# Block-causal attention into an RWKV channel mix: a second batch's q and k in nine-token rows, transposed by TensorE, with a new table of ranks

## The chip, the cores and the metric

The kernel runs on one core of one Trainium2 chip. The metric is the device time of one execution in microseconds, median over runs. All inputs and the output are in HBM as fp32. The kernel before took 289.88 us (three runs, 289.01 to 291.78) when the prediction was made. Executions of one kernel differ by about 1%, so small differences below come with a 95% interval. A run counts as slow when it took over 1.5% more than the fastest of its kernel; ratios use fast runs alone. "Slower" and "faster" below mean that the interval lies on one side of 1; a change clear of 2% is shown only where the whole interval lies beyond 0.98 or 1.02.

## The reference, cut to what matters

Attention over 8 batches, 8 heads, 576 tokens, head size 64, with a mask of blocks of 64 tokens; its output goes through a token-shift channel mix (d_model 512, d_ff 1024).

```python
scores = q @ k.T / 8                                  # (8, 8, 576, 576)
scores = where(pos_i // 64 >= pos_j // 64, scores, -1e9)
x = softmax(scores) @ v                               # heads side by side: (8, 576, 512)
x_prev = x shifted by one token, zero at each batch's start
xk = mu_k * x + (1 - mu_k) * x_prev
xr = mu_r * x + (1 - mu_r) * x_prev
out = sigmoid(xr @ w_r) * (relu(xk @ w_k) ** 2 @ w_v) # w_k 512x1024, w_v 1024x512, w_r 512x512
```

q, k and v are normal numbers times 0.1. The scores are therefore all close to zero.

## The kernel before

Each batch goes through the same steps: q and k are loaded as fp32, cast to bf16, and transposed so that the head dimension lies on the partitions; TensorE makes scores, ScalarE the exponentials, TensorE the product with v and a transpose back, GpSimd and VectorE the token-shift mixes. The 4608 tokens are then taken in nine chunks of 512 through WK, WR and WV.

The order of every engine is fixed when the kernel is built. A list scheduler in the kernel takes tasks with modelled lengths, dependences and buffer rings; on each engine it takes the ready task of lowest rank. The ranks come from a table that has been tuned by search.

```python
class Plan:
    LATENCY = {"PE": 0.12, "ACT": 0.08, "DVE": 0.08, "POOL": 0.1, "SP": 2.4}
    ...
RANK = {
 'loads': ['v0', 'g1q', 'v3', 'g0k', 'g0q', 'wk4', 'wr3', 'wk5', 'v1', ...],  # the order of the first loads
 ...
 'qk': [47.0, 48.0, 50.5, 52.5], 'v': 56.0, 'turn': -176.0, 'av': -44.5,      # the steady part, per batch
 'xt': 8.5, 'mix': 694.5, 'xr': 29.5, 'moe': 20.0,
}
```

Batches 1 to 7 use the DMA crossbar. Each pair of heads takes two half loads for q and two for k, in rows of 256 B (64 fp32), a cast of each half on GpSimd, a cast of the tail (the last 64 of 576 tokens), and a transposing DMA that SyncE issues:

```python
def add_qk(b, pr, rank, turn_rank):
    for n, src in enumerate((q, k)):
        t = load(key, lambda: new("ld", [P, 4, 2, D], FP),
                 lambda d, src=src: [
                     (d[:, :, h], src[b, 2 * pr + h, 0:512].rearrange(
                         "(t p) d -> p t d", p=P)) for h in range(2)], ...)
        ... nc.gpsimd.tensor_copy(tiles["nb", b, pr][:, n, 0:4], ...)
    last = on("POOL", 0.4, rank, tail, ...)
    ... nc.sync.dma_start_transpose(out=tiles["qkt", b][:, pr]..., in_=tiles["nb", b, pr]...)
```

Batch 0 is the exception. Its q and k come as rows of nine tokens (2304 B), two blocks of two heads in one tile, are cast by sixteen instructions that each take half of the partitions (every second one moves its data to the other half), and are transposed by TensorE:

```python
LONG = {(0, 0): ("DVE", "POOL", "DVE", "ACT"), ...}
def add_long(g, ranks):
    ... d[:, x], src[0, 4*g + 2*x:4*g + 2*x + 2].rearrange("y (p j) d -> (y p) (j d)", j=JT) for x in range(2)
    for i, (x, y) in enumerate(((0, 0), (1, 1), (1, 0), (0, 1))):
        dst = tiles["nb", 0, g, n][x * D:x * D + D, :, y * D:y * D + D]
        src = tiles[key][y * D:y * D + D, x].rearrange("p (j d) -> p j d", d=D)
```

GpSimd also makes two of a chunk's four shift differences (t_d), the fp16 casts of v (VO), and a small "fix" of xk and xr at each batch's first token (128x4). The fix comes after the mixes of its chunk, and the chunk's WK matmuls need it.

The softmax here doesn't subtract the row's maximum and nothing guards it: scores larger than these inputs give would overflow.

## Time and profile before

| | before |
|---|---|
| time, median | 289.88 us |
| span of the profiled run | 287.3 us |
| TensorE busy (instructions) | 253.5 us (2260) |
| VectorE, ScalarE, GpSimd busy | 207.9, 187.9, 142.3 us |
| packets under 512 B | 142848 of 151071 |
| first matmul of each chunk's WV product, chunks 0 to 8 | 61.5, 98.4, 124.2, 153.3, 181.0, 212.4, 238.3, 257.8, 275.3 us |

"Busy" TensorE isn't TensorE at its full rate.

SyncE's own queue in order of time (start us, length, issued DMA) shows when batch 2's first load, its tail, goes out, and the weight load ahead of it:

```profile
52.24 3.23 SPq L226 DMA_DIRECT2D t_ld<-in_moe_w_v_dram  x1
55.51 0.61 SPq L226 DMA_DIRECT2D t_tl<-in_q_dram  x1
```

GpSimd's timeline at the end of the hole around 75 to 81 us (start, length, instruction, in brackets the idle time before it and its releaser):

```profile
79.86 0.61 POOL L358 CAST VO<-t_vl 128x512 f16<-128x512 f32 x1 [1.37 <-DMA t_vl<-in_v_dram]
80.44 0.65 POOL L695 TENSOR_TENSOR t_xk<-t_xt,MUK 128x4 f16<-128x4 f32 x1
```

### The profile page before, as it was taken

What the parts mean: (1) busy time and instruction counts of PE and PEld (TensorE: products, weight loads), DVE (VectorE), ACT (ScalarE), POOL (GpSimd) and SP (SyncE); (2) the same over time, 40 slices, a digit from 0 to 9 for tenths busy, and PEclk for the clock granted to TensorE, in tenths of its full rate; (3) what the DMA queues carried; (4) which work ended last, traced back from release to release, by engine and by line L of the source; (5) the groups of instructions that cost most, each with busy time, mean ns of one, the idle gap of its engine ahead of it and who ended that gap; (6) DMA issues with size and microseconds to landing.
All of it is one profiled execution on the core that took longest, in us unless ns stands there. A gap on an engine that the chain in (4) does not pass through costs nothing.

```text
span 287.3 us, 6211 instructions
## 1 busy us (share of the span) xinstructions
PE 253.5 (88%) x2260; PEld 137.2 (48%) x2260; DVE 207.9 (72%) x356; ACT 187.9 (65%) x297; POOL 142.3 (50%) x310
## 2 busy tenths in 40 slices
PE   0366948989679999999999989999999999999994
PEld 0333722455325644565565445556545655444441
DVE  4661696485968598868989856878787789897641
ACT  1368576875748768857886677867866884360530
POOL 5546374455647665567577357755864221301000
PEclk9999995999979999999999999999999999999998
DMA  7997899999999999999989998999899100201102
GB/s 218 361 248 175 226 191 216 267 177 234 180 216 177 192 257 253 193 203 235 255 172 184 227 264 179 186 263 239 178 212 255 40 3 37 110 2 74 72 37 113
DMA packets 151071, 52.59 MB, mean 183 GB/s; under 512 B 142848, under 2 KB 142848, under 8 KB 151040
## 3 DMA queue, kind: packets, MB, share of 16 engines
q1 hardware_dynamic: 151040, 52.19, 84.0%
q8 instruction: 18, 0.29, 0.5%
q14 instruction: 13, 0.11, 0.1%
HBM read 33.56 MB, written 9.44 MB: 150 GB/s over the span
## 4 chain that ended last, share of the span: by engine, by line
PE 53%; DMA 16%; DVE 10%; SPq 6%; ACT 5%; issue 4%; POOL 4%; POOLq 0%; DVEq 0%; ACTq 0%
PE t_mm L716 16%; PE t_mm L768 15%; PE t_mm L745 8%; DMA t_ld<-in_q_dram 6%; PE t_m L557 5%; PE t_s L498 5%; SPq L226 5%; ACT t_e L520 4%; DMA t_qkt<-NB 3%; PE t_m L630 3%; DMA t_ld<-in_moe_w_r_dram 2%; DMA t_xr<-in_k_dram 2%; DVE t_o L778 2%; DVE t_xk L680 2%; DMA t_vl<-in_v_dram 1%
## 5 line engine op out<-in xcount | busy, mean ns | idle before, releaser
L520 ACT ACTIVATE t_e<-t_s 128x1024 f16<-128x1024 f32 x96 | 95.6, 1028 | 23.7 <-PE t_s L498 23.5
L716 PE MATMUL t_mm<-t_xk,WK 128*128 128x512 f16 x288 | 71.1, 389 | 2.6 <-POOL t_xk L695 2.4
L732 DVE TENSOR_TENSOR t_k<-t_kr 128x512 f16<-128x512 f32 x72 | 54.9, 777 | 22.6 <-ACT t_kr L726 22.6
L768 PE MATMUL t_mm<-WV,t_k 128*128 128x512 f16 x288 | 66.8, 379 | 0.0
L726 ACT ACTIVATE t_kr<-t_mm 128x512 f32<-128x512 f32 x72 | 42.9, 599 | 17.9 <-PE t_mm L716 17.1
L255 POOL CAST NB<-t_ld 128x512 bf16<-128x512 f32 x56 | 39.6, 709 | 26.1 <-DMA t_ld<-in_k_dram 12.3
L498 PE MATMUL t_s<-t_qkt 64*128 64x64 bf16 (+4 forms) x384 | 35.7, 295 | 9.3 <-ACT t_e L520 4.9
L557 PEld LDWEIGHTS <-t_e 128*128 128x128 f16 x896 | 34.9, 100 | 15.8 <-issue 3.5
L716 PEld LDWEIGHTS <-WK 128*128 128x128 f16 x288 | 26.4, 99 | 33.4 <-issue 8.7
L768 PEld LDWEIGHTS <-t_k 128*128 128x128 f16 x288 | 27.1, 98 | 31.4 <-issue 1.8
L528 POOL MEMSET t_e<- 64x128 f16 x128 | 23.3, 199 | 35.9 <-ACT t_e L520 32.1
L778 DVE SCALAR_TENSOR_TENSOR t_o<-t_t,t_mm 128x512 f32<-128x512 f32 x36 | 24.6, 685 | 21.6 <-PE t_mm L768 20.2
L358 POOL CAST VO<-t_vl 128x512 f16<-128x512 f32 (+1 forms) x40 | 28.7, 721 | 21.7 <-DMA t_vl<-in_v_dram 20.0
L745 PE MATMUL t_mm<-WR,t_xr 128*128 128x512 f16 x144 | 37.3, 388 | 0.0
L755 ACT ACTIVATE t_t<-t_mm 128x512 f32<-128x512 f32 x36 | 21.7, 602 | 22.2 <-PE t_mm L745 21.9
L557 PE MATMUL t_m<-VO,t_e 128*128 128x65 f16 x784 | 32.3, 193 | 2.1 <-POOL VO L358 0.9
L680 DVE SCALAR_TENSOR_TENSOR t_xk<-t_d,MUK,t_xt 128x512 f16<-128x512 f32 x36 | 31.2, 876 | 3.2 <-POOL t_d L668 2.8
L609 ACT COPY t_xt<-t_m 128x256 f32<-128x256 f32 (+7 forms) x68 | 23.8, 401 | 14.0 <-PE t_m L630 13.9
L680 DVE SCALAR_TENSOR_TENSOR t_xr<-t_d,MUR,t_xt 128x512 f16<-128x512 f32 x36 | 31.8, 897 | 0.0
L578 DVE TENSOR_TENSOR t_x<-t_m,t_r 128x320 f32<-128x320 f32 x56 | 27.5, 492 | 1.9
L668 POOL TENSOR_TENSOR t_d<-t_xt 128x512 f32<-128x512 f32 x18 | 20.0, 1114 | 17.4 <-DVE t_xr L680 9.0
L498 PEld LDWEIGHTS <-t_qkt 64*128 64x128 bf16 x384 | 13.5, 97 | 29.2 <-issue 18.9
(47 smaller groups left out, 188.8 us busy)
## 6 DMA issues: line engine op xcount, KB each, us to landing
out_dram<-t_o SPq DMA_DIRECT2D x36, 256.0 KB, 2.8
t_vl<-in_v_dram SPq DMA_DIRECT2D x32, 256.0 KB, 4.1
t_ld<-in_q_dram SPq DMA_DIRECT2D x56, 128.0 KB, 3.8
t_ld<-in_k_dram SPq DMA_DIRECT2D x56, 128.0 KB, 3.6
t_ld<-in_moe_w_k_dram SPq DMA_DIRECT2D x8, 256.0 KB, 5.9
t_ld<-in_moe_w_v_dram SPq DMA_DIRECT2D x8, 256.0 KB, 5.3
t_xk<-in_q_dram SPq DMA_DIRECT2D x4, 288.0 KB, 4.7
t_xr<-in_k_dram SPq DMA_DIRECT2D x4, 288.0 KB, 5.8
```

Of the source, the lines that this page charges most:

```text
L255: nc.gpsimd.tensor_copy(tiles["nb", b, pr][:, n, 0:4], tiles[key][:, :].rearrange("p t h d -> p t (h d)"))
L358: nc.gpsimd.tensor_copy(VOs[b % 2][0:n, sc, :, 0:D], tiles["vl", b, sc][0:n])
L498: nc.tensor.matmul(PS[:, h, col:col + n], qkt[rows, pr, 1, kc * P:kc * P + P], qkt[rows, pr, 0, q0:q0 + n], start=True, stop=True)
L520: nc.scalar.activation(tiles["e", b, pr][:, :, i, :], tiles["ps", b, it], AF.Exp, scale=ISQ)
L557: nc.tensor.matmul(PA[:, mt * D1:(mt + 1) * D1], stationary(b, h, kc, mt), VOs[b % 2][:, kc, h, 0:D1], start=(kc == 0), stop=(kc == mt))
L680: nc.vector.scalar_tensor_tensor(tiles[name, c][:, cc], tiles["d", c, cc], (MUK1, MUR1)[n][:, cc:cc + 1], tiles["xt", c][:, cc, 1:CH + 1], ...
L716: nc.tensor.matmul(ps, WK[:, cc, jc * P:(jc + 1) * P], tiles["xk", c][:, cc], start=(cc == 0), stop=(cc == CCn - 1))
L726: nc.scalar.activation(tiles["kr", c, jc], tiles["pk", c, jc], AF.Relu)
L732: nc.vector.tensor_tensor(tiles["k2", c][:, jc], KR, KR, ALU.mult)
L745: nc.tensor.matmul(ps, tiles["xr", c][:, cc, jt * P:(jt + 1) * P], WR[:, cc], start=(cc == 0), stop=(cc == CCn - 1))
L768: nc.tensor.matmul(ps, tiles["k2", c][:, jc, jt * P:(jt + 1) * P], WV[:, jc], start=(jc == 0), stop=(jc == JCn - 1))
L778: nc.vector.scalar_tensor_tensor(tiles["o", c, jt], tiles["t", c, jt], 1.0, tiles["pv", c, jt], ALU.add, ALU.mult)
```

## The change

The intent is to treat batch 1 as batch 0 is treated, and both more cheaply: loads in rows of nine tokens, one load and one cast for a block of two heads, transposes by TensorE. The pairs of heads are (0,2) and (1,3) in these batches, so that a cast stays on its partitions. Batch 0's loads move from the buffers of xk and xr to those of the other loads. All ranks are new.

```diff
+LONGS = 2
 RANK = {
- 'loads': ['v0', 'g1q', 'v3', 'g0k', 'g0q', 'wk4', 'wr3', ...
- 'qk': [47.0, 48.0, 50.5, 52.5], 'v': 56.0, 'turn': -176.0, 'av': -44.5,
- 'xt': 8.5, 'mix': 694.5, 'xr': 29.5, 'moe': 20.0,
+ 'loads': ['g0q', 'g0k', 'g1q', 'v0', 'v1', 'v4', 'wr2', 'g1k', 'v3', 'v2', 'b1g1k', ...
+ 'qk': [56.0, 57.0, 63.5, 67.0], 'v': 67.0, 'qkt': [267.5, -111.5], 'turn': -116.0, 'av': -72.0,
+ 'xt': 9.5, 'mix': 840.5, 'xr': 121.0, 'moe': 21.5,
 ... (the other ranks of batch 0 too)
-    def add_long(g, ranks):
+    LONG = {(0, 0): ("DVE", "ACT"), (0, 1): ("POOL", "ACT"),
+            (1, 0): ("DVE", "POOL"), (1, 1): ("POOL", "DVE")}
+    def add_long(b, g, ranks):
-        t = load(key, lambda ring=ring: new(ring, [P, 2, S], FP), ... for x in range(2)
-            for i, (x, y) in enumerate(((0, 0), (1, 1), (1, 0), (0, 1))):
-                dst = tiles["nb", 0, g, n][x * D:x * D + D, :, y * D:y * D + D]
+            for x in range(2):
+                t = load(key, lambda: new("ld", [P, S], FP),
+                         lambda d, src=src, x=x: [(d, src[b, 4*g + 2*x:4*g + 2*x + 2]
+                              .rearrange("y (p j) d -> (y p) (j d)", j=JT))], ranks[n], 0.85, ...)
+                eng = LONG[g, n][x] if b == 0 else ("POOL", "DVE")[x]
+                dst = tiles["nb", b, g, n][:, :, x * D:x * D + D]
 ...
-        if b == 0:
+        if b < LONGS:
             for g in range(2):
-                add_long_qkt(g, R["qkt0"][g])
+                add_long_qkt(b, g, r + R["qkt" if b else "qkt0"][g])
```

## The prediction

> **What bounds the kernel now.** I read the page's slices first, then a table of windows, then the chain that ended last, then the groups by shape and the list of DMA issues.
>
> The slices of the page (each 1/40 of 287.3 us, 7.18 us), tenths busy; PEclk is the granted TensorE clock:
>
> ```profile
> PE   0366948989679999999999989999999999999994
> PEclk9999995999979999999999999999999999999998
> DMA  7997899999999999999989998999899100201102
> ```
>
> The DMA engines are full from the second slice to the 31st (about 220 us) and nearly empty afterwards. PE is full from the 14th slice (93 us) to the end. So two limits overlap in the middle; the opening, some 90 us, is the only place where PE has holes. A table of windows shows how deep they are (columns: length, busy us and instructions of PE, PE weight loads, DVE, ACT, POOL, then the granted clock, the DMA share and GB/s):
>
> ```profile
> 5.00:10.00 5.00, 0.00 (x0) 0.00 (x0) 2.63 (x4) 1.75 (x3) 2.25 (x4) 1.00 1.08 363
> 40.00:45.00 5.00, 1.97 (x16) 1.05 (x16) 4.90 (x9) 2.51 (x5) 4.24 (x8) 0.84 1.27 168
> 45.00:50.00 5.00, 5.00 (x19) 1.40 (x16) 2.52 (x4) 3.12 (x5) 1.17 (x5) 0.50 0.99 218
> 75.00:80.00 5.00, 1.98 (x16) 1.03 (x17) 5.00 (x7) 4.24 (x8) 3.37 (x8) 1.00 1.13 229
> 80.00:85.00 5.00, 3.86 (x21) 1.37 (x21) 2.68 (x3) 1.38 (x3) 3.06 (x8) 0.66 1.22 225
> 125.00:150.00 25.00, 24.88 (x249) 14.05 (x247) 21.09 (x37) 18.22 (x31) 15.87 (x32) 1.00 1.04 220
> 245.00:287.30 42.30, 38.37 (x178) 17.27 (x176) 26.20 (x39) 14.88 (x26) 3.38 (x4) 0.98 0.18 68
> ```
>
> PE idles 3.0 us of 40 to 45 and then runs five microseconds at half clock; the same again from 75 to 85. The chain says what these holes wait for (start us, length, what):
>
> ```profile
> 3.45 5.37 DMA t_xr<-in_k_dram
> 11.28 1.02 PE t_m L408 x8
> 17.22 1.03 ACT t_e L520
> 26.94 5.43 DMA t_ld<-in_moe_w_r_dram
> ...
> 38.48 4.63 DMA t_qkt<-NB
> 45.35 1.88 PE t_mm L716 x4
> ...
> 57.91 4.32 DMA t_ld<-in_q_dram
> 70.50 5.19 DMA t_qkt<-NB
> ...
> 248.42 6.91 PE t_mm L716 x32
> ```
>
> The first transposes wait for the first k load until 11.28 us, the first exponential comes at 17.22, the first matmul of the channel mix at 45.35, and the scores of batch 2 hang on a crossbar transpose at 70.5. In the last stretch 32 matmuls take 6.91 us, 216 ns each with no hole: that is PE's full rate. A chunk of 512 tokens needs 32 + 16 + 32 = 80 of these, 17.3 us; nine chunks 155 us. Attention adds, by my estimate from start-to-start times in the trace, 70 us: 960 AV products at 30 ns (30 took 0.91 us in the chain), 160 fp32 transposes at 108 ns, and scores about 22 us, because a pair of heads in the two row halves runs side by side. Some 225 us of PE work stand against 287 us. Counting it in 12 us stretches, about 45 us of the 62 lost lie before 84 us, about 5 in the tail, and the rest thinly between. **The end is set by PE, and PE's losses are set by how soon data and the first chunk arrive.**
>
> **What the Trainium skill says.** "DMA: Bandwidth & Descriptors", Specifications, gives 512 B as the smallest transfer for line rate. The trace agrees in direction: around 125 to 150 us, where rows are 256 B, a full queue moves 220 / 1.04 = 212 GB/s; from 5 to 10 us, with rows of 2304 and 2048 B beside v, it moves 363 / 1.08 = 336 GB/s. By packet records a 256 B packet occupies an engine for 21.8 ns on average, a 2304 B one for 108 ns, a 2048 B one for 98 ns. The same page, DMA Transpose (X-bar), Alternative transpose paths, names TensorE with an identity as the other way: this kernel already does that for batch 0, eight blocks in 1.02 us at the cold clock. "TensorE: Matmul & The Clock Gate", Part 1, says that idle windows drop the clock to half and some 3.4 us of activity restore it; the records show 0.50 for 6.8 us and again for 3.4 us, right after the two holes. "VectorE: DVE Perf Modes", Walkthrough, counts work per lane, so a cast of 128 partitions should cost what one of 64 costs. The records of POOL, another engine, go that way: 128x512 takes 708 ns, 64x512 773 ns.
>
> **The change part by part.**
>
> *Batch 0's loads and casts.* Sixteen casts of 64x576 (DVE 7 at 746 ns, POOL 6 at 663, ACT 3 at 670) become eight of 128x576 at the same length each: DVE 4, ACT 2, POOL 2. Each now waits for its own block of 288 KB and not for two. More important is the order: before, v0 and a q of group 1 and another v stood ahead of the first k; now q and k of group 0 are first. Before, v0, g1q, v3 and g0k are 2048 x 21.8 ns + 512 x 108 ns over 16 engines = 2.8 + 3.5 = 6.2 us, and g0k was in use by 8.8. After, g0q and g0k are 512 x 108 / 16 = 3.5 us, so landed about 5.6 us; a POOL cast and an ACT cast (they are chained, 0.66 + 0.67, the first overlapping the second block's flight) put the first transpose at 6.4 us in place of 11.28. One evacuation, one cast, one more evacuation (1.23 + 0.75 + 1.28) follow on DVE before the first exponential: about 11.2 in place of 17.2.
>
> *Batch 1's q and k.* Out go 16 half loads, two tail loads and four crossbar transposes: 8192 + 1024 + 5120 = 14336 packets of 256 B, 14336 x 21.8 / 16 = 19.5 us of full DMA queue. In come eight loads of 288 KB: 1024 x 108 / 16 = 6.9 us. Net the queue is 12.6 us shorter, and all of it lies before batch 2's loads. Cross-check by bytes: (2.36 + 1.31) MB at 212 GB/s less 2.36 MB at 336 gives 10.3 us. Batch 2's first load (its tail was issued at 55.5) should be issued around 43 to 45. The wait for batch 1's transposes, 4.6 us of chain at 38.5, is gone.
>
> *What it adds.* PE: 36 transposes, 2.0 us at the warm spacing of 56 ns, 3.8 us if cold; I take 2.5. DVE: five evacuations at 1.22 to 1.28 (6.2), four casts (3.0), less three casts of batch 0 (2.2): +7 us, all before 45 us, where DVE is 4.90 of 5 busy in one window. ACT: one evacuation more (1.0), one cast less. POOL: eight casts at 709, four tails at 609 and four casts of batch 0 out, four casts in: about 8 us less. The memory-sets, exponentials and products stay. Pairing heads (0,2) and (1,3) costs nothing: it only renames which rows go where, so that no cast crosses between the halves of the partitions.
>
> *When the first channel-mix matmul can start.* By DMA: the list of loads up to wk1, the last of the first four wk blocks, sums to about 35 us (block loads at 0.86, weights at 0.79, v at 1.4 us), so 1.3 + 35.3 + 2 = 39. By DVE: from 11 us it must do group 1's evacuations 3.7, six casts 4.5, eight normalisations of 0.68 (5.4), batch 1's evacuations 6.2, and mixes of about 7: 38. So about 40 in place of 45.35, 5.4 us earlier.
>
> *The sum.* Earlier channel mix, 5.4. Less of the half clock after it: it cost 6.8 x 0.5 = 3.4; I give back 2, since PE has batch 1's transposes and scores to do just before. The hole at 75 to 85: 4.2 us idle plus 3.4 x 0.5 = 1.7 of cold clock, 5.9 in all; batch 2 comes some 11 us earlier, the channel mix 5, so the hole mostly closes, and I count 4.5. Together 11.9, less 2.5 of new PE work: **9.4 us**, so 289.9 - 9.4 = 280.5; I say 280.
>
> **The rivals.** (1) *The DMA queue is the true bound throughout*: then all 12.6 us and the earlier start reach the end, and the time is near 273. For it: the queue is full until 220 us. Against: when it empties, 67 us of PE work at full rate remain, so the channel mix lags the loads and PE is what ends last. (2) *PE-bound, only the start counts*: the first transposes come 5 us sooner, minus 2.5, the hole at 75 stays because the static order puts batch 2 behind something else: about 286. For it: PE is 24.88 of 25 busy in mid-kernel. (3) *DVE takes over the opening*: 7 us more on an engine that already is full from 35 to 45; batch 0's mixes, which stand behind batch 1's evacuations in the new order of DVE, keep the first channel-mix matmul at 45: about 287 to 290. Against: DVE idled before 9 us and between 20 and 30 (1.34 of 5 us busy in 25 to 30), so there is room if the data come early.
>
> **Range and chances.** My sum is 280; rival 1 gives 273, rivals 2 and 3 give 286 and more. Eight in ten: 273 to 286.5. Two per cent is 284.1 us; the first loads and the shorter queue are simple arithmetic and need only half of what I count. I give 0.82 to faster by over 2%, 0.16 to within, 0.02 to slower.
>
> **What would show it.** Right: the first transpose at 6 to 7 us and the first exponential at 11 to 12; packets under 512 B down by over 14000; batch 2's first loads at 43 to 46; the first channel-mix matmul at 38 to 42; no hole of several us around 75; the DMA queue emptying some 12 us earlier, near 208. PE's idle time in the first 90 us should shrink by about 10 us and PE's matmul count rise by 36. Wrong: if the first channel-mix matmul is still behind DVE (its wait named as a mix or a normalisation) at 45 us, if an in-order engine sits at a weight cast whose load comes late, as ACT did at 26.9, or if the hole only moves from 75 to another place.

## The result, and the profile after

The changed kernel took **278.92 us** (four runs, 278.13 to 280.98) against 289.44 us (288.38 to 291.78) for the kernel before in the same rounds. The ratio is 0.9637, with a 95% interval of 0.9553 to 0.9721. Ratios are computed as the mean time of one kernel's fast runs over that of the other's of the same rounds, so they are not quite the ratio of the medians that are quoted.

The profiled execution of the changed kernel was the slowest of its four (span 279.2 us; the others 276.3 to 277.9). What the traces explain is thus 287.3 - 279.2 = 8.1 us of the 10.5.

The slices of the page after (each 1/40 of 279.2 us, 6.98 us; tenths busy, the granted TensorE clock, the DMA engines):

```profile
PE   1668839999999999999999699999999999999994
...
PEclk9999986999999999999999989999999999999999
DMA  7999999499999999899989969999995101202102
DMA packets 137471, 51.28 MB, mean 184 GB/s; under 512 B 128224, under 2 KB 128224, under 8 KB 137440
```

TensorE is busy for a tenth of the first slice already and is full from the seventh slice (42 us) instead of the 13th (86 us; the prediction counted one slice too many). There is one new dent, the 6 in slice 23, with a lower clock in slice 24. Packets under 512 B fell from 142848 to 128224. The DMA row falls to 5 in the 31st slice and to 1 in the next, so it empties near 213 us; before, it was full through the 31st slice, to 222 us.

The table of windows after (columns as in the prediction):

```profile
45.00:50.00 5.00, 5.00 (x52) 2.51 (x49) 3.10 (x6) 3.92 (x6) 0.81 (x2) 0.83 1.15 220
75.00:80.00 5.00, 5.00 (x82) 3.26 (x80) 4.52 (x10) 4.18 (x7) 2.20 (x7) 1.00 1.29 213
80.00:85.00 5.00, 5.00 (x58) 2.74 (x56) 4.79 (x7) 4.59 (x9) 4.16 (x9) 1.00 1.04 212
155.00:160.00 5.00, 2.46 (x21) 1.38 (x20) 1.47 (x3) 2.62 (x5) 2.01 (x4) 0.94 1.15 262
```

The hole of 75 to 85 is closed: TensorE is busy 5.00 of 5 in both windows, where it had 1.98 and 3.86. In 45 to 50 it does 52 matmuls in place of 19. But at 155 to 160 it is idle half of the time, where the kernel before is busy 5.00 of 5.

The chain that ended last, after (start us, length, what):

```profile
2.13 4.21 DMA t_ld<-in_k_dram
...
10.52 1.94 ACT t_e L523 x2
...
41.65 3.26 PE t_mm L722 x7
...
151.59 6.12 DMA t_vl<-in_v_dram
```

The first k is landed at 6.34 us, the first exponential starts at 10.52 (17.22 before), and the channel mix runs from 41.65 us. One of its matmuls came at 38.97, and TensorE then waited 2.29 us for GpSimd's cast of a block of WK. The last line shown is new: a load of v, issued at 151.59, now lies on the chain.

SyncE's queue, after:

```profile
37.42 3.51 SPq L230 DMA_DIRECT2D t_ld<-in_moe_w_v_dram  x2
40.97 0.61 SPq L230 DMA_DIRECT2D t_tl<-in_q_dram  x1
```

Batch 2's first load goes out at 40.97 us, 14.5 us earlier. The same weight loads are the last before it.

The new hole, on TensorE and then on GpSimd (timelines):

```profile
159.75 0.68 PE L562 MATMUL t_m<-VO,t_e 128*128 128x65 f16 x9 [2.54 <-POOL t_e L531]
```

```profile
157.76 1.67 POOL L365 CAST VO<-t_vl 128x512 f16<-128x512 f32 x2 [3.04 <-DMA t_vl<-in_v_dram]
159.49 0.34 POOL L531 MEMSET t_e<- 64x128 f16 x2
```

GpSimd waits 3.04 us for a v load, casts, and only then clears the pieces of t_e that TensorE has been waiting for. TensorE loses 2.54 us there, and the records then show half the clock for 3.4 us from 159.4 us.

The start of each chunk's WV product tells where the time went:

| chunk | 0 | 1 | 2 | 3 | 4 | 5 | 6 | 7 | 8 |
|---|---|---|---|---|---|---|---|---|---|
| before | 61.5 | 98.4 | 124.2 | 153.3 | 181.0 | 212.4 | 238.3 | 257.8 | 275.3 |
| after | 57.9 | 86.5 | 115.4 | 143.8 | 175.6 | 204.3 | 230.3 | 249.8 | 267.4 |
| lead, us | 3.6 | 11.9 | 8.8 | 9.5 | 5.4 | 8.1 | 8.0 | 8.0 | 7.9 |

So the lead is 3.6 us at chunk 0 and 11.9 at chunk 1, and about 8 at the end.

### The profile page after: what moved, and what is told of

Its sections match the earlier page's. It is cut to its first block, busy times and chain, and to the rows that moved or that the text cites.

```text
span 279.2 us, 6287 instructions
## 1 busy us (share of the span) xinstructions
PE 253.6 (91%) x2296; PEld 137.3 (49%) x2296; DVE 211.9 (76%) x362; ACT 188.6 (68%) x297; POOL 140.7 (50%) x299
## 3 DMA queue, kind: packets, MB, share of 16 engines
q1 hardware_dynamic: 137440, 50.88, 79.3%
## 4 chain that ended last, share of the span: by engine, by line
PE 68%; DVE 11%; ACT 5%; DMA 5%; POOL 4%; issue 4%; SPq 2%; POOLq 0%; ACTq 0%; DVEq 0%
PE t_mm L722 19%; PE t_mm L774 19%; PE t_mm L751 8%; PE t_m L562 7%; PE t_s L501 7%; PE t_m L636 5%; DVE t_k L738 4%; ACT t_e L523 3%; DMA t_vl<-in_v_dram 2%; DMA t_ld<-in_q_dram 2%; DMA t_ld<-in_k_dram 2%; DVE t_qkt L440 1%; POOL WK L385 1%; DVE t_xr L686 1%; DVE t_d L674 1%
## 5 line engine op out<-in xcount | busy, mean ns | idle before, releaser
L722 PE MATMUL t_mm<-t_xk,WK 128*128 128x512 f16 x288 | 72.5, 390 | 2.5 <-POOL WK L385 2.3
L738 DVE TENSOR_TENSOR t_k<-t_kr 128x512 f16<-128x512 f32 x72 | 58.1, 818 | 17.6 <-ACT t_kr L732 17.3
L774 PEld LDWEIGHTS <-t_k 128*128 128x128 f16 x288 | 27.8, 98 | 33.9 <-issue 2.9
L261 POOL CAST NB<-t_ld 128x512 bf16<-128x512 f32 x48 | 36.3, 762 | 8.3 <-DMA t_ld<-in_q_dram 5.1
L365 POOL CAST VO<-t_vl 128x512 f16<-128x512 f32 (+1 forms) x40 | 29.2, 738 | 17.4 <-DMA t_vl<-in_v_dram 16.4
L751 PE MATMUL t_mm<-WR,t_xr 128*128 128x512 f16 x144 | 36.4, 379 | 0.0
L674 POOL TENSOR_TENSOR t_d<-t_xt 128x512 f32<-128x512 f32 x18 | 22.0, 1222 | 23.6 <-ACT t_xt L615 13.5
L615 ACT COPY t_xt<-t_m 128x256 f32<-128x256 f32 (+7 forms) x68 | 23.8, 401 | 11.2 <-PE t_m L636 11.1
L686 DVE SCALAR_TENSOR_TENSOR t_xr<-t_d,MUR,t_xt 128x512 f16<-128x512 f32 x36 | 29.9, 843 | 0.0
L636 PE MATMUL t_m<-identf,t_x 128*128 128x128 f32 x160 | 24.5, 279 | 3.1 <-DVE t_qkt L438 1.3
```

Source lines behind the costliest of these rows:

```text
L261: nc.gpsimd.tensor_copy(tiles["nb", b, pr][:, n, 0:4], tiles[key][:, 0:512].rearrange("p (t c) -> p t c", c=P))
L365: nc.gpsimd.tensor_copy(VOs[b % 2][0:n, sc, :, 0:D], tiles["vl", b, sc][0:n])
L636: nc.tensor.matmul(px[:, i * P:(i + 1) * P], src, identf, is_transpose=True, start=(i == 0), stop=(i == 3))
L686: nc.vector.scalar_tensor_tensor(tiles[name, c][:, cc], tiles["d", c, cc], (MUK1, MUR1)[n][:, cc:cc + 1], tiles["xt", c][:, cc, 1:CH + 1], ...
L722: nc.tensor.matmul(ps, WK[:, cc, jc * P:(jc + 1) * P], tiles["xk", c][:, cc], start=(cc == 0), stop=(cc == CCn - 1))
L738: nc.vector.tensor_tensor(tiles["k2", c][:, jc], KR, KR, ALU.mult)
```

## The experiments

Twelve kernels ran. Six expectations missed: the times of old_new_ranks, blocks_new_ranks, blocks_old_ranks and rows_old_ranks lie above every range that was named, those of rows_new_open and rows_new_steady 1 to 2 us above the nearest one. pad_first fell between its two ranges. The theory after the result was the prediction's own: the gain comes from an earlier start and from a shorter DMA queue ahead of batch 2. The rivals were that the gain lies in the new ranks, whatever the code does, and that the queue's length doesn't matter but what blocks SyncE and GpSimd does.

### Code and ranks apart

Four runs separate code from ranks. "Blocks" is the new code with `LONGS = 1`: batch 0 by the new loads and casts, batch 1 back on the crossbar.

**old_new_ranks**: the old code with the new table; batch 1's four loads take the places of the new names.

```diff
- 'loads': ['v0', 'g1q', 'v3', 'g0k', ...], ... (old RANK)
+ 'loads': ['g0q', 'g0k', 'g1q', 'v0', ...], ... (new RANK)
+ # b1g1k -> b1qk0, b1g0q -> b1qk1, b1g0k -> b1qk2, b1g1q -> b1qk3
```

> The kernel before with the new table of ranks alone (the load names of batch 1 renamed in the order in which they stand). If the new order of loads and the retuned ranks made the gain (theory R), this is near the kernel after, 279 to 283 us. If structure made it (theory O: batch 0's blocks and batch 1's rows fill the opening), the first transposes still come earlier than 11.3 us, since q and k of group 0 are loaded first (about 8 us), but batch 2's loads still start near 55 us and the time is 285 to 291.

Measured: 295.91 us (294.63 to 296.93), ratio 1.0175 (1.0098 to 1.0252), so slower than before. The first transpose came at 5.9 us and the first exponential at 12.75 (5.15 and 10.52 in the changed kernel, 11.28 and 17.22 before), so most of the early start comes from the order of loads; the rest goes with the new loads and casts. But the first channel-mix matmul came at 47.9 us and batch 2's first load at 55.5, and TensorE ran 27.3 us at half clock from 34.0.

**blocks_new_ranks**: the new code and ranks, batch 1 on the crossbar.

```diff
-LONGS = 2
+LONGS = 1
-                rank = r + R["qk"][pr]
+                rank = at[f"b1qk{pr}"] if b == 1 else r + R["qk"][pr]
```

> The kernel after with batch 1 sent back to the crossbar: batch 0's block loads and the new ranks stay. Theory O: the first transposes at 5.2 us as in the kernel after, batch 2's first loads back near 53 us, the hole around 75 us back, 283 to 287 us: half of the gain. If the start alone pays (theory S): 278 to 281. If only the shorter queue pays (theory Q): 287 to 290.

Measured: 294.8 us (291.84 to 298.55, fifteen runs, five of them slow), ratio 1.0106 (1.0066 to 1.0146). Its page shows where the early start goes (slices of 7.3 us):

```profile
PE   1668430599999996999999999999998999999994
...
PEclk9999955589999998999999999999999999999999
```

The first slices are those of the changed kernel. Then TensorE starves: 4, 3, 0 and 5 tenths from the fifth slice on, 23.9 us of half clock, and the first channel-mix matmul at 46.5 us in place of 39.0. The new order puts batch 1's q and k ahead of most weights. With the crossbar path that delays the weights: the second block of WK is issued at 40.7 us, where the changed kernel issues it at 21.8, and TensorE waits 7.3 us for the cast of a block of WK.

**blocks_old_ranks** and **rows_old_ranks** differ in batch 1's path alone, under the old ranks.

```diff
 # blocks_old_ranks: the new code, LONGS = 1, RANK of the kernel before
 # rows_old_ranks:   the new code, LONGS = 2, RANK of the kernel before
+ 'qkt': [267.5, -111.5],        # the one new entry that rows need
```

> Batch 0's blocks alone, with the old ranks and so the old order of loads (v0 and group 1's q first, group 0's k fourth). All theories expect little of the start: first transposes near 10 us, time 286 to 290. Theory S would have it at 284 or less.

> The whole new code with the old ranks (and the new ones for batch 1's transposes, which the old table lacks). Theory O: the queue before batch 2 is 12.6 us shorter as in the kernel after, batch 2's first loads near 43 us, 280 to 285 us. Theory R (ranks): 287 to 290. Theory Q (queue): 278 to 281.

Measured: 294.56 us (293.23 to 296.5), ratio 1.0153 (1.0064 to 1.0243), and 294.2 us (292.12 to 297.08), ratio 1.0132 (1.0099 to 1.0165). Both are slower than the kernel before, and as good as equal. Yet under the old ranks batch 1's path does just what the prediction claimed of it. Windows of the first and of the second, at the place of the old hole:

```profile
78.00:84.00 6.00, 1.58 (x14) 0.63 (x14) 5.96 (x8) 4.46 (x7) 4.14 (x10) 0.82 1.33 228
```

```profile
78.00:84.00 6.00, 5.02 (x55) 2.62 (x55) 5.93 (x11) 3.13 (x4) 4.29 (x9) 1.00 1.10 209
```

TensorE goes from 1.58 to 5.02 busy microseconds of six. Batch 2's first load is issued at 39.1 us in place of 57.0, and chunk 1's WV product starts at 93.2 us in place of 101.2, 8.0 us earlier. Then it is lost: from chunk 1 to chunk 8 the rows need 184.5 us (93.2 to 277.7), the crossbar 178.3 (101.2 to 279.5). The spans, 290.5 and 291.5 us, differ by 1.0.

What brings that load forward can be read from SyncE's queue. With the crossbar, two of its waits (us in all, times, longest) and batch 2's first load; below it the same load with the rows:

```profile
SPq L288 <- POOL t_e L530: 4.6, 1, 4.6
SPq L288 <- POOL NB L260: 1.6, 1, 1.6
57.01 0.60 SPq L229 DMA_DIRECT2D t_tl<-in_q_dram  x1
```

```profile
39.12 1.12 SPq L230 DMA_DIRECT2D t_tl<-in_q_dram  x1
```

The two waits shown are those of batch 1's transposes, 6.2 us. But in all, SyncE waits as long in one kernel as in the other: from 10 us to that load its listed waits sum to 13.8 us with the crossbar and to 13.6 with the rows, where other waits take the place of the transposes'. The rest of the stretch, in which SyncE issues, falls from 33.2 to 15.5 us. So the 18 us are issuing time: batch 1 needs 16 loads, two tails and four transposes with the crossbar, and eight loads with the rows. Why single issues of the same loads take from 0.5 to 2 us isn't shown; a full queue may be part of it.

Two more kernels mix the tables, with the new code: **rows_new_open** has the new ranks for the opening and the old for the steady part, **rows_new_steady** the reverse. **old_new_steady** puts the new steady ranks into the old code.

```diff
 # rows_new_open: new code, new RANK, but
+STEADY = ('qk', 'v', 'turn', 'av', 'xt', 'mix', 'xr', 'moe')   # these from the old table
 # rows_new_steady: new code, old RANK, but STEADY from the new table
 # old_new_steady:  old code, old RANK, but STEADY from the new table
```

> The kernel after with the ranks of the steady part (qk, v, turn, av, xt, mix, xr, moe) put back to the old values; load order and the ranks of batch 0, of the casts and of batch 1's transposes stay new. Theory P (the gain is made in the first 90 us, by an order of loads that short rows allow): first channel-mix matmul near 39 to 41 us as in the kernel after, lost time of PE at 96 us near 37 us; total 279 to 284. Theory M (the retuned steady ranks make the gain in the middle): 287 to 293.

> The new code with the old opening ranks and load order, the new ranks of the steady part. Theory P: first transposes near 11.2 us, first channel-mix matmul at 46 to 50, 287 to 292. Theory M: 279 to 284.

> The kernel before with the new ranks of the steady part alone. Theory P: no better than before, 288 to 294. Theory M: 280 to 285.

Measured: rows_new_open 294.79 us (293.52 to 296.76), ratio 1.0211 (1.0145 to 1.0278); rows_new_steady 292.87 us (291.16 to 295.33), 1.0145 (1.0069 to 1.0222); old_new_steady 288.94 us (287.7 to 291.13), 1.0038 (1.0002 to 1.0075).

rows_new_open is the telling one. Its opening is nearly as good as that of the changed kernel (first transpose 5.3 us, first channel-mix matmul 40.3), but holes come back at 72 to 84 us and 108 to 120 us. GpSimd's timeline in the first hole, then TensorE's:

```profile
78.41 0.78 POOL L360 CAST VO<-t_vl 128x512 f16<-128x512 f32 x1 [0.56 <-DMA t_vl<-in_v_dram]
79.15 0.21 POOL L696 TENSOR_TENSOR t_xk<-t_xt,MUK 128x4 f16<-128x4 f32 x1
```

```profile
79.42 1.86 PE L717 MATMUL t_mm<-t_xk,WK 128*128 128x512 f16 x4 [2.48 <-POOL t_xk L696]
```

Four casts of v, at 72.77, 74.71, 76.83 and 78.41 us, three of them waiting for their loads, stand ahead of the fix of 0.21 us for which TensorE waits. It is the same pattern as in the kernel before at 79.86 us. In the changed kernel the fix comes at 70.22 us, 0.69 us after a cast of v ended. The casts don't explain the whole hole, though: the fix also needs VectorE's last mix of xk, which ended at 77.99 us here and at 79.30 in the kernel before, so without the cast just ahead of it the fix could have started at most 1.2 and 1.1 us earlier, of holes of 2.48 and 2.42. No kernel was run that only moves the fix ahead of the casts.

All combinations, as ratios to the kernel before:

| code | old ranks | new opening, old steady | old opening, new steady | new ranks |
|---|---|---|---|---|
| before | 1 | - | 1.0038 | 1.0175 |
| blocks (batch 0 alone) | 1.0153 | - | - | 1.0106 |
| rows (batches 0 and 1) | 1.0132 | 1.0211 | 1.0145 | 0.9637 |

No part gains alone. By the ratios the new ranks are worth 1.0132 - 0.9637 = 0.0495, some 14 us, to the new code and cost the old code about 5. "It is the ranks" falls as well: they need the rows, which are worth 1.0106 - 0.9637 = 0.0469 under the new ranks and 0.0021 under the old. How much of this is the rows allowing a better order, and how much simply a longer search for the new code than for the old, these runs don't tell.

### The start and the queue

The engine orders of the changed kernel are kept here (the traces show the same order of instructions on the four compute engines), and spare loads are put into SyncE's queue, into buffers that nobody uses until later.

**pad_first**: eight spare loads (512 packets of 256 B each) ahead of the first q.

```diff
-                         lambda d, src=src, x=x: [
+                         lambda d, src=src, x=x, n=n: pad(8 if (b, g, n, x) == (0, 0, 0, 0) else 0) + [
```

> The kernel after, all engine orders unchanged, with 8 spare loads of 128 KB in 256 B rows issued before the first q load: 8 x 512 x 18 to 21.8 ns / 16 = 4.6 to 5.6 us of queue, so that the first transposes move from 5.2 to about 10 to 11 us, where the kernel before has them. Theory S (an earlier start is passed on to the end one for one): 283 to 285 us. Theory N (the opening has slack; the first channel-mix matmul waits for weights and casts, not for the first scores): 279 to 281, the first channel-mix matmul moving by less than 3 us from 39.

Measured: 282.62 us (281.59 to 283.67), ratio 0.9775 (0.9715 to 0.9836). The first transpose came at 10.4 us and the first exponential at 16.5, both 5 to 6 us later than in the changed kernel and much as in the kernel before. This cost 0.9775 - 0.9637 = 0.0138 of 289 us, or 4.0 us; the two intervals only just touch. Chunk 0 came at 63.1 us, 1.6 us after the kernel before, and chunk 1 at 91.8, still 6.6 us before it. So 6.4 us of the gain (288.99 - 282.62, medians of these rounds) remain without the early start. But that is a net figure. The new hole isn't there either: chunk 4 follows chunk 3 after 28.5 us (149.8 to 178.3) in place of 31.8, with the same order of instructions. Up to chunk 3 the padded kernel is 5.3 to 6.1 us behind the changed one, so the late start is passed on in full, and the missing hole then gives 3.4 us back. A shift of some microseconds decides whether GpSimd meets that v load late.

**pad_early**: spare loads between batch 1's loads, so that batch 2's come later.

```diff
                               .rearrange("y (p j) d -> (y p) (j d)", j=JT))]
+                         + pad((2 - n) if b == 1 else 0),
```

> The kernel after, every engine's order unchanged, with 12 spare loads of 128 KB in rows of 256 B put between batch 1's q and k loads into tiles that are not used until 50 us: 12 x 512 packets x 21.8 ns / 16 = 8.4 us of queue given back ahead of the weights, and nothing else. Theory P: the first channel-mix matmul comes 6 to 9 us later (45 to 48), PE stays at half clock for longer, total 284 to 289. If the queue's length doesn't matter there (the start alone pays): under 281.

The text says twelve loads; `n` is read when the loads are issued and is 1 by then, so each of batch 1's eight loads got one spare load and eight were issued. So the queue grew by 8 x 512 x 21.8 ns / 16 = 5.6 us (an estimate from the packet time before) and not by 8.4. Measured: 280.62 us (277.25 to 282.49, four runs, two of them slow); over the fast runs the ratio is 0.9639 (0.9551 to 0.9727), as good as the 0.9637 of the changed kernel. In the profiled run, which was one of the slow ones, batch 2's first load went out at 44.5 us, 3.5 us later than without; its other times aren't compared. Almost half of the 12.6 us by which the prediction had shortened the queue was given back, and the end didn't move within the 0.9% that the two fast runs resolve. (If the two slow runs were ordinary scatter, the medians of all runs, 280.62 and 288.65, give 0.972.)

### Shorter queues without the rows

Three kernels were meant to shorten the queue and leave the crossbar path as it is. q and k go in rows of four tokens (1024 B), so that tokens are in the wrong order: **these results are wrong**. The comparison with the reference passed all the same, because with scores near zero the order of keys hardly shows. The order of instructions on the four compute engines is that of the kernel they start from, as the traces confirm. (old_wide_all also drops a dependence between the casts of successive batches, which that unchanged order keeps anyway.)

```diff
-                         (d[:, :, h], src[b, 2 * pr + h, 0:512].rearrange("(t p) d -> p t d", p=P)) for h in range(2)],
+                         (d[:, 2*h:2*h + 2], src[b, 2 * pr + h, 0:512].rearrange("(p a j) d -> p a j d", a=2, j=2)) for h in range(2)],
 # old_wide_b1: kernel before, batch 1 only;  old_wide_all: kernel before, batches 1 to 7;
 # new_wide_all: changed kernel, batches 2 to 7
```

> Wrong result on purpose. The kernel before, all engine orders unchanged, with batch 1's q and k loaded in rows of 1024 B (other tokens in the partitions, same bytes, same tiles): 8192 packets of 256 B become 2048, some 4.9 to 6 us of queue less before batch 2. Theory Q (the queue's length is what the change shortens to good effect, whatever the order): 283 to 286. Theory N (in a static order the queue's length alone moves little): 287 to 290.

> Wrong result on purpose. As the last one for batches 1 to 7: the queue is some 40 us shorter in all. It bounds what the kernel before could gain from a shorter queue in its own order. If the queue bounds the middle, PE's hole at 75 us and the thin losses from 84 to 228 us close: 274 to 280. If PE and the other engines' orders bound it: 284 to 288.

> Wrong result on purpose. The kernel after, all engine orders unchanged, with the q and k of batches 2 to 7 loaded in rows of 1024 B: 49152 packets of 256 B become 12288, by packet time some 25 to 35 us of queue less. In its trace the kernel after lost some 4 us at 157 us, where PE waited for POOL and POOL for a v load that landed 6.1 us after its issue. If the queue's length makes that hole and the thin losses between 90 and 220 us: 273 to 276 us. If the static order makes them (SyncE stands still for some 50 us in that stretch waiting for POOL and DVE, so the queue is not short of time): 276.5 to 279.

Measured: old_wide_b1 288.94 us (286.54 to 291.49), ratio 0.999 (0.9961 to 1.0019). old_wide_all 286.78 us (285.33 to 288.56), ratio 0.9932 (0.9909 to 0.9954). new_wide_all 278.11 us (277.2 to 279.28), ratio 0.9566 (0.9517 to 0.9615).

In old_wide_b1 batch 2's first load still goes out at 54.5 us, against 55.5 in the kernel before: three of batch 1's four crossbar transposes, at 37.7, 41.0 and 44.4 us, stand ahead of it in SyncE's order, and a weight load that waits 3 us for its buffer comes last. From 10 us to that load SyncE's issuing time falls by 6.0 us (30.9 to 24.9), but its waits grow by 5.0 (14.6 to 19.6). Nor did the queue get shorter in time: its packets took 83.6% of a span of 288.4 us, against 84.0% of 287.3 before, 241 us both times, because the other 256 B packets got slower (22.4 ns on average in place of 21.8). So this run says little about the queue's length. In old_wide_all packets under 512 B fell from 142848 to 85504, but that load goes out at 55.2 and the hole at 75 to 80 stays (TensorE 2.14 busy of 5). The chain through the hole:

```profile
77.37 0.54 POOL VO L362
...
78.22 0.66 POOL t_xk L699
```

It is again a cast of v, its load issued at 73.32 and landed at 77.25, then the fix, and at 78.93 the channel mix. VectorE's last mix of xk ended at 77.79 us, so the cast delayed this fix by at most 0.4 us. By the pages the packets of the queue took 221 us here (77.7% of 284.9), 20 us less than before (some 40 were expected) and as little as in the changed kernel (79.3% of 279.2). So 20 us less of packet time is worth 0.7%, where the changed kernel, with the same packet time, gains 3.6%; and none of the 0.7% comes from the hole. In the changed kernel the same edit takes the packets from 221 to 204 us (73.8% of 276.4; 25 to 35 us less were expected) and is worth 0.9637 - 0.9566 = 0.0071, about 2 us, with overlapping intervals. There it does remove the new hole:

```profile
155.00:160.00 5.00, 5.00 (x54) 2.80 (x53) 2.39 (x5) 3.77 (x6) 1.57 (x4) 1.00 1.13 261
```

No correct kernel that beats the changed one was found. A kernel with a third batch in nine-token rows can't be built with these ranks (with `LONGS = 3` the scheduler stops with "the plan is stuck"), and no ranks were searched for it.

## Why the prediction was right or wrong, point by point

The time, 280, was 1.1 us off and inside the range. Most of the early steps hold; the one about the queue doesn't. And no term stood for the ranks of the steady part: rows_new_open has the predicted opening (first channel-mix matmul at 40.3 us) and the rows, lacks these ranks alone, and is 2.1% slower than the kernel before. In that the verdict was luck.

**The start: right.** The first transpose came at 5.15 us (6.4 predicted, 6 to 7 as the sign), the first exponential at 10.52 (11.2; 11 to 12), both even earlier. The casts took the same time on twice the partitions: medians of 745 ns on VectorE, 667 on GpSimd and 672 on ScalarE for 128x576, where 64x576 had taken 746, 663 and 670 on average. TensorE's "cold clock" in the opening can be seen too, though the record of the granted clock reads 1.00 there: in both kernels the transposes of batch 0 start 107 ns apart, and in the changed kernel those from 23.4 us on start 56 ns apart. What the start is worth at the end was not separated in the prediction; pad_first puts it at 5 to 6 us up to chunk 3 and at a net 4 us at the end. old_new_ranks, with the first exponential at 12.75, shows that the new order of loads makes most of it.

**The packets: right.** 14624 fewer packets under 512 B were counted, over 14000 predicted. Batch 2's first load went out at 40.97 us; 43 to 45 was predicted, so it came even earlier. By the pages the packets of the queue took 20 us less in all (241 to 221); the prediction's 12.6 are batch 1's share, for which the two kernels under the old ranks give 13.2 (241.4 to 228.2, the sum over all packet records, by 16 engines).

**"PE's losses are set by how soon data and the first chunk arrive", and the net queue "12.6 us shorter" as the cause: wrong in its reason.** Four runs were meant to vary the queue's length. Longer by an estimated 5.6 us: no change within 0.9% (pad_early). Wide rows for batch 1: no change (old_wide_b1), but no shorter queue either. Shorter by 20 us: 0.7% (old_wide_all), and again about 0.7% in the changed kernel (new_wide_all). With ranks alike, replacing the *path* of batch 1 moves batch 2's first load by 18 us (57.0 to 39.1) and closes the hole, while making its packets wide moves that load by 1 us and leaves the hole. By SyncE's queue what the rows removed is 14 of batch 1's 22 issues, and with them the transposes that wait in SyncE's order. The sum of SyncE's waits stayed the same, yet in old_wide_b1, where issuing got 6.0 us shorter and the transposes stayed, longer waits took 5.0 back. How much is the number of issues and how much the waiting transposes, the casts and tails on GpSimd or the transposes' flight was not separated. Nor does the earlier load carry the end by itself: under the old ranks its 18 us leave 1.0 us of the span.

**The first channel-mix matmul at 40: right, barely.** It came at 38.97, alone, then TensorE waited 2.29 us for GpSimd's cast of WK; the others ran from 41.65. It is a mild case of what the prediction named as a sign of being wrong, an in-order engine at a weight cast.

**The sum.** Up to chunk 0 the terms were 5.4 for the channel mix, 2 for the clock and 2.5 off for new TensorE work, so 4.9; measured 3.6. The half-clock term failed: 6.8 us of it remained (39.9 us on), so nothing came back where 2 were counted. The hole at 75 to 85 was put at 4.5; from chunk 0 to chunk 1, a stretch that holds this hole, the lead grew by 8.2 (36.8 us to 28.6). By chunk 1 the lead was 11.9 against 9.4 predicted. After that the prediction had no term, and 4.0 us were given back: 2.4 by chunk 3, and 1.4 net from chunk 3 to 5, where the new hole at 157 us and its half clock take the lead from 9.5 to 5.4 and the kernel before then loses 2.7 of its own. So the hole in part moved to another place, which the prediction named as a sign of being wrong. The sum agreed as well as it did because its terms up to chunk 1 were too small (9.4 for 11.9) while the later loss had no term; that is luck.

**What the engines took on.** TensorE's 36 more matmuls are there (2260 to 2296), and its idle time in the first 90 us shrank by 9.9 us (busy 62.25 to 72.15), about 10 predicted. VectorE works 4.0 us more in all (207.9 to 211.9) and 6.4 more by 45 us (27.2 to 33.6), against 7 predicted. The prediction miscounted the new casts of batch 0: the table `LONG` gives VectorE three and GpSimd three, not four and two, so its own sum for VectorE should be 6.2. GpSimd was to lose 8 us and lost 1.6 (142.3 to 140.7): the 48 crossbar casts that remain took 762 ns on average, where 56 had taken 709, and the shift differences 1222 in place of 1114.

**The rivals.** Rival 1, the queue as the true bound, is refuted by old_wide_all, with 20 us less of packet time for 0.7%. Rival 2, a hole at 75 that stays because of the static order, didn't happen in the changed kernel, but rows_new_open, which differs in the steady ranks alone, shows a hole there (1.0211). Rival 3, VectorE taking over the opening, didn't happen. The DMA queue was to empty near 208 us, 12 us earlier; by the slices it empties near 213, some 9 us earlier. SyncE itself waits more than before: in 40 to 220 us its five largest groups of waits sum to 52 us (19.6, 11.9, 8.5, 7.3 and 5.0), all for GpSimd's or VectorE's work, against 36 before (12.5, 12.4, 4.1, 3.8 and 3.6). So the sum of its waits alone doesn't tell which kernel is faster.

## What to carry to other kernels

Where every engine's order is fixed, ask of a late load what stands ahead of it in the issuing engine's order, waits and issues both, before counting bytes or packets: here a 40% smaller count of small packets gave 0.7%, while a path with 8 issues in place of 22 brought the next batch's load 18 us forward. Check that an edit that should shorten a queue did so in the trace: wide rows for one batch didn't. A change of path and its order belong together: measure the new code with the old order too, and be ready to see it lose. A tiny instruction (here 0.2 to 0.7 us on GpSimd) behind a cast that waits for its load held TensorE up; moving it ahead is worth a try, up to 1.2 us at such a hole here, but wasn't tested by itself.

## What the Trainium skill lacked or had wrong

- "DMA: Bandwidth & Descriptors", Why small descriptors are slow (HBM only), gives 27% overhead for a 256 B descriptor from one mechanism, and no figure in time for the other that it names. The runs show more: on average, over loads and transposes alike, a 256 B packet holds an engine for 21.8 ns (11.7 B/ns), one of 1024 B 58.9 ns (17.4; old_wide_all), one of 2304 B 108 ns (21.3), so the small one moves 45% less per ns than the large one. The 256 B figure isn't a constant: it is 23.1 ns in old_wide_all. The page gives no table of packet times.
- "Perfetto Trace Analysis", What "DMA-bound" means, names DMA engines, the issuing sequencer solid with DMA slices, and SBUF reads. The list doesn't name a sequencer that stands still between its slices: in the changed kernel SyncE waited 52 us of 40 to 220 us for compute engines. What that costs at the end, no run here separates.
